# Delta in four operations, Q blocks from spread columns, 64-column scores and a new order of the first group in an attention backward kernel

## The chip, the cores and the metric

The kernel runs on one core of a Trainium2 chip. The metric is the device time of one execution in microseconds. The engines are PE (matrix multiplications, with weight loads listed apart as PEld), VectorE (DVE in the profile), ScalarE (ACT), GpSimd (POOL, which here issues the stores) and SyncE (SP, which issues the loads). Each engine works through its own instructions in order and waits on semaphores for the others.

## The reference

Two weights sets, A (attention over a cache) and B (an MLP), are each applied twice to the same small state x of shape 2 x 1 x 1024, and all gradients are returned:

```python
def _A_ref(x, k_cache, v_cache, wq, wo):        # Hq = 32, Hkv = 4, Sk = 16384, Dh = 128
    q = (x @ wq).reshape(B, Sq, Hq, Dh) ...
    scores = jnp.einsum("bhqd,bhkd->bhqk", q, k) * (Dh ** -0.5)
    p = _softmax(scores, axis=-1)
    o = jnp.einsum("bhqk,bhkd->bhqd", p, v)
    return (...o...) @ wo
...
    x = x + _A_ref(_layernorm(x), A_k_cache, A_v_cache, A_wq, A_wo)
    x = x + _B_ref(_layernorm(x), B_w1, B_b1, B_w2, B_b2)
    x = x + _A_ref(_layernorm(x), A_k_cache, A_v_cache, A_wq, A_wo)
    x = x + _B_ref(_layernorm(x), B_w1, B_b1, B_w2, B_b2)
    return x
...
_out, _vjp = jax.vjp(_f, A_x, A_k_cache, A_v_cache, A_wq, A_wo, B_w1, B_b1, B_w2, B_b2)
_grads = _vjp(grad_out)
```

For each of the 8 pairs of batch and KV head (a group, g) there are 8 query rows. The backward pass of attention needs, per layer, dO of the group, delta = the sum over the head of dO x O, ds = p x (V dO - delta), dq from ds and K, and the gradients dV = p dO and dK = ds q. dV and dK of the two layers are added and written once. The key and value caches and their gradients are 32 MB each.

## The kernel before

The kernel goes forward through both layers, then backward through layer 1 (`attn_bwd`, 500 to 662 us), and then through the MLP and attention of layer 0. The last part, from 731 us on, does layer 0's scores and dq and, for both layers together, dV and dK. It is the part that most of the change touches.

**Tiles.** A group has 16384 keys, cut into 4 chunks of 1 MB for K and 4 for V; a chunk is [128 partitions, 32 keys t, 128]. Chunk i of the last part is `chunks[i] = (group, c)`; `order` gives the groups, and the first one, `order[0]`, is group 7, whose K and V chunks were kept in SBUF (`held_tiles`, V already transposed). `e_all` holds the exponentials of both layers.

**Scores** (L1271). For 8 keys t, a transposed tile of V is the weight and the 16 columns of dO (two layers x 8 rows, `cols["V"]`) are streamed; the result goes to 16 places of a PSUM bank `dp` that lie 32 apart. A chunk has 32 such matmuls.

**ds** (`ds0`, L1276). One matmul of 512 columns with the weight `hot3` adds -delta to all of `dp`: `dlr` holds -delta as bf16 parts in three partitions, and `hot3` has ones in these three. VectorE then multiplies by `e_all` into `dX`.

**delta** (L859 to L882). VectorE multiplies dO by O, a matmul with ones sums over the partitions and gives the sum to every partition, and eight VectorE operations split it in three bf16 parts and put part i in partition i.

**Q blocks** (`make_qm`, L1211). For dV and dK, a weight block is a transposed piece of `e_all` or `dX`, and the streamed side is Qm, [128, 2 x 128], in which the 16 columns of dO or q are spread so that row 32r + 2k + t has column k in half t. PE transposes the 16 columns, VectorE copies them to `r16sb`, two matmuls with the constant `sel` spread them, and a copy brings them to SBUF. **`kv_pair`** (L1231) then makes half a chunk of dV or dK: 8 matmuls into four banks (`mx`), four copies out (`evac_cast`), and after the second half a store.

**dq** (`dq_quad`, L1297): 8 matmuls, four at a time in different columns of the array, with ds as weight and K streamed, into an accumulator. `evac` and `reduce` close a group.

**Banks and copies.** PSUM has two banks for transposes (`tp`), four for `mx`, one `sm` and one accumulator. `pick()` (L148) gives each copy out of PSUM to ScalarE or VectorE, by a planner's running charge of both; `charge` books other work.

**Order.** The program order of each engine is written by hand. After dO of layer 0 (`do_scaled`, L843; its products are ready at 731.5 us) the first group runs as a straight list (L1355 to L1388), then a loop over m (L1396) takes two slots of 8 keys x 128 per turn: transposes of V, scores two slots behind, `kv_pair`s for dK and dV, `make_blks`, a scheduled dq, and units of weight gradients (`step_fill`). Before, the list read: scores 1, delta's matmul, kv pair V 0, scores 2, delta, kv pair, scores 0, ds 1, scores 3, kv pair V 1, ds 0 and 2, dq of chunk 0, kv pair, ds 3, zeroing of two transpose banks (`fixed_tp`), K's Q block, dq of chunks 1 to 3. Loads wait in `pump` for tiles that are read or stored (`by_read`, `by_store`).

The w1 pass of layer 0 (`w_pass`, L1030) has a `mid` call that stands in PE's and VectorE's queues at its fifth chunk, at about 698 us.

Of the kernel before, what the change touches and what calls it, by code (L numbers as in the profile page):

```python
# [13 lines left out]
ALU = mybir.AluOpType  # L14
# [9 lines left out]
def kernel(  # L24
# [96 lines left out]
    sel = const.tile([16, 2, 4, 16, 2], BF16, name="sel")  # L121
    V.memset(sel[:], 0.0)
    for t in range(2):
        for r in range(4):
            V.tensor_copy(out=sel[:, t, r, :, t], in_=ident[0:16, 0:16])

# [5 lines left out]
    V.tensor_reduce(out=m3[:], in_=identf[:, 0:3], axis=AX.X, op=ALU.add)  # L132
# [701 lines left out]
    def attn_out_bwd(l, gT):  # L834
        V.tensor_copy(out=gA_all[:, :, lsl(l)], in_=gT[:])
        _, dops = w_pass(A_wo, HD, D, "do_ps", gT_bf=gA_all[:, :, lsl(l)])
        doT_bf = saved[f"a{l}"]["doT_bf"] = vec.tile([128, G, 8], BF16, name=f"doT_bf{l}")
        dof = do_scaled(l, dops)
        do_store(l, dof[:], doT_bf[:])
        delta(l, delta_mm(l, dof))  # L840
        return doT_bf

    def do_scaled(l, dops, ahead=None, half=lambda b, dof: None):  # L843
        sv = saved[f"a{l}"]
        dof = wrk.tile([128, G, 8], F32, name="dof")
        for b in (1, 0):
            V.tensor_tensor(out=dof[:, b * HKV:(b + 1) * HKV, :].rearrange("p k r -> p (k r)"), in0=dops[:, :, b],
                            in1=sv["rbc"][:, b * HKV:(b + 1) * HKV, :].rearrange("p k r -> p (k r)"), op=ALU.mult)
            if ahead is not None:
                r_ = sv["rbc"][:, b * HKV:(b + 1) * HKV, :].rearrange("p k r -> p (k r)")  # L850
                V.tensor_tensor(out=dof[:, b * HKV:(b + 1) * HKV, :].rearrange("p k r -> p (k r)")[:, 4:FJ:5],
                                in0=ahead.dp[:, :, b], in1=r_[:, 4:FJ:5], op=ALU.mult)
            half(b, dof)
        return dof
# [4 lines left out]
    def delta_mm(l, dof, bank=None):  # L859
        sv = saved[f"a{l}"]  # L860
        prod = wrk.tile([128, G, 8], F32, name="dprod")
        V.tensor_tensor(out=prod[:], in0=dof[:], in1=sv["oT"][:], op=ALU.mult)
        bank = pm_([128, 512], F32, "dl_ps") if bank is None else bank
        PE.matmul(bank[:, 0:G * 8], lhsT=onesf[:], rhs=prod[:].rearrange("p g r -> p (g r)"), start=True, stop=True)
        return bank

    def delta(l, bank):
        dlp = bank[:, 0:G * 8]
        rest_ = wrk.tile([128, G * 8], F32, name="dl_rest")
        V.tensor_scalar(out=rest_[:], in0=dlp, scalar1=-1.0, scalar2=None, op0=ALU.mult)  # L870
        part = wrk.tile([128, G * 8], BF16, name="dl_part")
        dst = dlr[:, :, l, :].rearrange("p g r -> p g r")
        as_g = lambda ap: ap.rearrange("p (g r) -> p g r", r=8)
        for i in range(3):
            V.tensor_copy(out=part[:], in_=rest_[:])
            if i == 0:
                V.tensor_scalar(out=dst, in0=as_g(part[:]), scalar1=identf[:, 0:1], scalar2=None, op0=ALU.mult)
            else:
                V.scalar_tensor_tensor(out=dst, in0=as_g(part[:]), scalar=identf[:, i:i + 1], in1=dst, op0=ALU.mult,
                                       op1=ALU.add)  # L880
            if i < 2:
                V.tensor_tensor(out=rest_[:], in0=rest_[:], in1=part[:], op=ALU.subtract)  # L882
# [138 lines left out]
    for w in "VK":  # L1021
        cols[w] = vec.tile([128, G, 2, 8], BF16, name="cols" + w)
        for k in range(2):
            if w + str(k) != "V0":
                V.tensor_copy(out=cols[w][:, :, k, :], in_=saved["a%d" % k]["qT_bf" if w == "K" else "doT_bf"][:])
    dq0 = vec.tile([128, G, 8], F32, name="dqT0")
# [5 lines left out]
                                  make_blks(0, None), make_blks(1, None)))  # L1032
# [176 lines left out]
    qms = {}  # L1209

    def make_qm(w, g):  # L1211

        rps = mtp()
        PE.transpose(rps[0:16, 0, :], cols[w][:, g].rearrange("p l r -> p (l r)"), ident[:])
        r16 = small.tile([16, 128], BF16, name="r16sb")
        V.tensor_copy(out=r16[:], in_=rps[0:16, 0, :])

        def second():
            Qm = wrk2.tile([128, 2, 128], BF16, name="Qm" + w)
            qps = mx()  # L1220
            for t in range(2):
                PE.matmul(qps[:, t * 128:(t + 1) * 128], lhsT=sel[:, t].rearrange("p r k t -> p (r k t)"), rhs=r16[:],
                          start=True, stop=True)
            evac_cast(Qm[:].rearrange("p a b -> p (a b)"), qps[:, 0:256], 256)
            qms[w, g] = Qm

        return second
# [43 lines left out]
    def scores(i, b, kT, dp):  # L1271
        do01 = cols["V"][:, chunks[i][0]].rearrange("p l r -> p (l r)")
        for j in range(8):
            PE.matmul(dp[:, :, b * 8 + j], lhsT=kT[:, j, :], rhs=do01, start=(b + j == 0), stop=False)
# [77 lines left out]
    def sm_dp():  # L1352
        return pm_([128, 16, TC], F32, "dp")[:]

    dof = do_scaled(0, pairs(dops, HQ), wob,  # L1355
                    lambda b, dof: do_store(0, dof[:, b * HKV:(b + 1) * HKV], cols["V"][:, b * HKV:(b + 1) * HKV, 0, :]))
    qv = make_qm("V", order[0])
    odp = {1: kept_scores(1, sm_dp())}
    dl_bank = pt([128, 512], F32, "dl")
    delta_mm(0, dof, dl_bank)  # L1360
    qv()
    kv_pair("V", 0, 0)
    odp[2] = kept_scores(2, tp_dp())
    delta(0, dl_bank)
    charge("D", 2.0)
    kv_pair("V", 0, 1)
    odp[0] = kept_scores(0, tp_dp())
    ds0(1, odp[1])
    odp[3] = kept_scores(3, sm_dp())
    kv_pair("V", 1, 0)  # L1370
    for c in (0, 2):
        ds0(c, odp[c])
    for q in range(2):
        dq_quad(0, q)
    kv_pair("V", 1, 1)
    ds0(3, odp[3])
    TP.extend(fixed_tp(i) for i in range(2))
    banks["tp"] = lambda: nxt("tp", TP)
    qk = make_qm("K", order[0])
    for c in (1, 2):  # L1380
        for q in range(2):
            dq_quad(c, q)
    qk()
    for q in range(2):
        dq_quad(3, q)
# [10 lines left out]
    while 2 * m < NS + 12 or late or fill or late_pe or m <= max(v_at) + 2:  # L1396
# [6 lines left out]
        for k in range(2):  # L1403
            s = 2 * m + k
            if s < NS:
                i, b = NCH + s // NB, s % NB
                cv = get("V", *chunks[i])[:].rearrange("p (t d) -> p t d", d=128)
                kT = ktp.tile([128, 8, 128], BF16, name="kT", tag="kT")
                tp = mtp()
                for j in range(8):  # L1410
                    PE.transpose(tp[:, j, :], cv[:, b * 8 + j, :], ident[:])  # L1411
                evac_bf16(kT[:].rearrange("p a b -> p (a b)"), tp[:].rearrange("p a b -> p (a b)"), 1024)
                kTs[s] = kT
                if b == NB - 1:
                    done("V", *chunks[i])
            if 0 <= s - 2 < NS:
                score0(s - 2)
# [46 lines left out]
```

## Time and profile before

| | |
|---|---|
| median of 9 runs | 1151.3 us (1146.68 to 1153.17) |
| the profiled execution | 1151.3 us |
| its span | 1149.5 us |
| mean granted TensorE clock | 0.834 |
| busy: PE, VectorE, ScalarE, GpSimd | 83%, 55%, 49%, 6% of the span |
| moved | 449.30 MB, mean 391 GB/s |

The page is of one execution. Busy shares are over the whole span. "PEclk" is the clock that TensorE was granted, 1.00 being full speed. The DMA share is the mean busy share of the core's 16 DMA engines. In a list of instructions in order of time, the first number is the start in us from the span's start, the second the duration, then engine, line, operation, output and inputs, shapes and count; a bracket gives the idle time before the instruction on its engine and what ended it. The end of a matmul is modelled, so a PE that is shown busy is not always one at its peak.

### The profile page before, as it was taken

Reading aid. Unit: us, or ns where it says so; the run is one execution under the profiler, and the core shown is the slowest. Engines: PE = TensorE matmul, PEld = TensorE weight load, DVE = VectorE, ACT = ScalarE, POOL = GpSimd, SP = SyncE. Lnnn points to the kernel's source line nnn. Section 1 sums busy time; section 2 is a strip of 40 time slices with the busy share of each in tenths; the row PEclk is TensorE's granted clock in tenths of the full one; section 3 lists DMA queues with packets and bytes.
Section 4 is the critical chain, followed back from the end, with each engine's and each line's share of the span. In section 5 each row is a group of like instructions: output and inputs, shape, how many; then the busy total and the mean of one; then the engine's idle time right before and its main releaser. Section 6 shows DMA issues by size and latency. Waiting matters only on the chain. (4 is left out here: it accounts for less than half of the span.)

```text
span 1149.5 us, 39958 instructions
## 1 busy us (share of the span) xinstructions
PE 953.5 (83%) x17581; PEld 727.6 (63%) x17581; DVE 632.1 (55%) x1335; ACT 567.2 (49%) x1417; POOL 63.9 (6%) x113
## 2 busy tenths in 40 slices
PE   4988886488879976899987799788898999998885
PEld 3867774487767755887775688665555555555552
DVE  1535441133535423454845365668777877787684
ACT  0544351022535420344454455657677867786673
POOL 0000000000000000000000000001111112111111
PEclk9979785597989876899998799888758867797695
DMA  8999999998999989999899899877999999999996
GB/s 371 424 424 424 424 424 412 409 361 363 424 424 424 423 328 423 405 355 411 345 420 421 324 370 351 323 291 291 397 402 408 422 422 420 424 422 420 423 423 260
DMA packets 89130, 449.30 MB, mean 391 GB/s; under 512 B 7026, under 2 KB 7026, under 8 KB 49788
## 3 DMA queue, kind: packets, MB, share of 16 engines
q1 hardware_dynamic: 72204, 348.17, 74.9%
q0 software_dynamic: 16752, 98.59, 20.7%
q8 instruction: 137, 2.24, 0.7%
q14 instruction: 37, 0.30, 0.1%
HBM read 348.14 MB, written 98.58 MB: 389 GB/s over the span
## 5 line engine op out<-in xcount | busy, mean ns | idle before, releaser
L158 ACT COPY kT<-tp 128x512 int32<-128x512 int32 x209 | 122.7, 588 | 257.5 <-PE tp L424 248.7
L161 DVE COPY kT<-tp 128x1024 bf16<-128x1024 bf16 x159 | 108.6, 690 | 109.6 <-PE tp L424 96.4
L424 PE MATMUL tp<-ident,kv_K 128*128 128x128 bf16 x1728 | 142.8, 231 | 4.0 <-DMA kv_K<-in_A_k_cache_dram 3.8
L424 PEld LDWEIGHTS <-kv_K 128*128 128x128 bf16 x1728 | 108.4, 103 | 4.7 <-DMA kv_K<-in_A_k_cache_dram 4.5
L169 DVE CAST big<-xm 128x512 bf16<-128x512 f32 x142 | 92.4, 685 | 29.9 <-PE xm L1242 12.9
L166 ACT CAST big<-xm 128x512 bf16<-128x512 f32 x155 | 84.6, 592 | 26.5 <-PE xm L1144 15.6
L577 PEld LDWEIGHTS <-kT 128*128 128x128 bf16 x2048 | 76.3, 98 | 28.1 <-issue 21.7
L577 PE MATMUL sc<-qT_bf,kT 128*128 128x8 bf16 x2048 | 91.8, 171 | 0.7 <-issue 0.7
L424 PE MATMUL tp<-ident,kv_V 128*128 128x128 bf16 x864 | 69.7, 226 | 13.6 <-DMA kv_V<-in_A_v_cache_dram 11.6
L274 PE MATMUL wtp<-ident,wt 128*128 128x128 bf16 x928 | 75.3, 228 | 3.9 <-issue 2.4
L541 ACT ACTIVATE e_all<-sc,negm 128x64 bf16<-128x64 f32 x256 | 77.1, 345 | 1.3 <-DVE negm L536 1.2
L310 PEld LDWEIGHTS <-wt 128*128 128x128 bf16 x1696 | 48.9, 103 | 43.8 <-issue 15.1
L169 DVE CAST keepK<-xm 128x512 bf16<-128x512 f32 x95 | 61.6, 684 | 15.5 <-PE xm L1242 9.8
L456 PE MATMUL acc_all<-kv_V,e_all 128*16 128x256 bf16 x864 | 46.3, 294 | 25.6 <-DMA kv_V<-in_A_v_cache_dram 13.1
L161 DVE COPY wT<-wtp 128x1024 bf16<-128x1024 bf16 (+1 forms) x64 | 40.5, 637 | 47.3 <-PE wtp L274 44.2
L158 ACT COPY wT<-wtp 128x512 int32<-128x512 int32 (+1 forms) x60 | 34.5, 575 | 63.4 <-PE wtp L274 48.3
L166 ACT CAST keepK<-xm 128x512 bf16<-128x512 f32 x102 | 54.8, 592 | 22.2 <-PE xm L1242 21.5
L424 PEld LDWEIGHTS <-kv_V 128*128 128x128 bf16 x864 | 54.8, 101 | 15.4 <-DMA kv_V<-in_A_v_cache_dram 12.3
L166 ACT CAST keepV<-xm 128x512 bf16<-128x512 f32 (+1 forms) x98 | 53.0, 592 | 21.9 <-PE xm L1242 18.7
L274 PEld LDWEIGHTS <-wt 128*128 128x128 bf16 x928 | 57.8, 102 | 4.7 <-issue 3.4
L541 ACT ACTIVATION_READ_ACCUMULATOR e_all<-sc,negm 128x1 f32 x256 | 60.2, 235 | 0.0
L169 DVE CAST keepV<-xm 128x512 bf16<-128x512 f32 (+1 forms) x74 | 47.9, 684 | 16.6 <-PE xm L1242 12.6
(352 smaller groups left out, 1777.8 us busy)
## 6 DMA issues: line engine op xcount, KB each, us to landing
kv_K<-in_A_k_cache_dram SPq DMA_DIRECT2D x81, 1024.0 KB, 12.2
kv_V<-in_A_v_cache_dram SPq DMA_DIRECT2D x81, 1024.0 KB, 12.2
out_dram<-big POOLq DMA_DIRECT2D x36, 1024.0 KB, 16.7
wt<-in_A_wo_dram SPq DMA_DIRECT2D x32, 1024.0 KB, 10.8
wt<-in_B_w_dram SPq DMA_DIRECT2D x32, 896.0 KB, 14.0
out_dram<-keepK POOLq DMA_DIRECT2D x22, 1024.0 KB, 16.8
out_dram<-keepV POOLq DMA_DIRECT2D x18, 1024.0 KB, 15.9
wt<-in_A_wq_dram SPq DMA_DIRECT2D x16, 1024.0 KB, 8.7
```

The costliest lines, as they stand in the source:

```text
L158: S.copy(out=dst.bitcast(I32), in_=src.bitcast(I32))
L161: V.tensor_copy(out=dst, in_=src)
L166: S.copy(out=dst, in_=src)
L169: V.tensor_copy(out=dst, in_=src)
L274: PE.transpose(tp[:, o, :], wv[:, j, (o0 + o) * 128:(o0 + o + 1) * 128], ident[:])
L310: PE.matmul(fps[:, jo, :].rearrange("p (a b) -> p a b", b=2), lhsT=wv[:, j, jo * 128:(jo + 1) * 128], rhs=xT_bf[:, j0 + j, :].unsqueeze(1) ...
L424: PE.transpose(tp[:, j, :], cv[:, b * 8 + j, :], ident[:])
L456: PE.matmul(self.acc[cg:cg + 16, :], lhsT=coef(u), rhs=self.cv[:, t:t + 2, :].rearrange("p t d -> p (t d)"), start=False, stop=True, tile_ ...
L541: S.activation(out=e_all[:, g, f * half:(f + 1) * half, l, h, :], in_=sc[g][f][:, h, :].rearrange("p (a b) -> p a b", b=2), func=ACT.Exp, ...
L577: PE.matmul(sc[g][f][:, :, t % TH], lhsT=kT[:, j, :], rhs=q_bf[:, g, :], start=True, stop=True)
```

## The change

Delta is split by four VectorE operations in place of eight: every partition gets the first part, partitions 64 to 127 are overwritten with the second, and 96 to 127 with the third; `hot3` has its ones in partitions 0, 64 and 96. For layer 0 it is done in two halves of the groups, the second half first.

A Q block is made from the columns spread by VectorE into a zeroed tile `spr` (two copies), used as the weight of two matmuls with the identity. The transpose, `r16sb` and `sel` are gone. K's block of the first group, and what is known of V's, are made inside the w1 pass (`q_parts`).

Scores stream 64 columns: a tile `wide_do` has the 16 columns of dO at every seventh place with zeros around them, and each matmul of key t writes a run of four keys, of which it adds zero to three. Two such tiles alternate by group; a copy per group fills one.

The first group's list is reordered: the dq of a chunk follows its ds, between the kv pairs, and the other half of delta is made near the end.

```diff
-    V.tensor_reduce(out=m3[:], in_=identf[:, 0:3], axis=AX.X, op=ALU.add)
+    V.tensor_reduce(out=m3[:], in_=identf[:, 64:128:32], axis=AX.X, op=ALU.add)
+    V.tensor_tensor(out=m3[:], in0=m3[:], in1=identf[:, 0:1], op=ALU.add)
...
-    def delta(l, bank):
-        dlp = bank[:, 0:G * 8]
-        rest_ = wrk.tile([128, G * 8], F32, name="dl_rest")
...
-        for i in range(3):
-            V.tensor_copy(out=part[:], in_=rest_[:])
...
+    def delta(l, bank, gs=slice(0, G)):
+
+        dlp = bank[:, 8 * gs.start:8 * gs.stop].rearrange("p (g r) -> p g r", r=8)
+        rest_ = wrk.tile([128, G, 8], F32, name="dl_rest")[:, gs]
+        dst = dlr[:, gs, l, :]
+        V.tensor_scalar(out=dst, in0=dlp, scalar1=-1.0, scalar2=None, op0=ALU.mult)
+        V.scalar_tensor_tensor(out=rest_, in0=dlp, scalar=-1.0, in1=dst, op0=ALU.mult, op1=ALU.subtract)
+        V.tensor_copy(out=dst[64:128], in_=rest_[64:128])
+        V.tensor_tensor(out=dst[96:128], in0=rest_[96:128], in1=dst[96:128], op=ALU.subtract)
...
+    for w in "VK":
+        spr[w] = wrk.tile([128, 258], BF16, name="spr" + w)
+        nc.gpsimd.memset(spr[w][:], 0.0)
+
+    def q_spread(w, gcols, k0, n):
+        diag = spr[w][:].rearrange("p (t x) -> p t x", x=129)[:, :, 0:128].rearrange(
+            "p t (r k z) -> p t r k z", r=4, k=16)[:, :, :, k0:k0 + n, 0]
+        for t in range(2):
+            V.tensor_copy(out=diag[:, t], in_=gcols.unsqueeze(1).to_broadcast([128, 4, n]))
+
+    def q_make(w, g, bank):
+        Qm = wrk2.tile([128, 2, 128], BF16, name="Qm" + w)
+        for t in range(2):
+            PE.matmul(bank[:, t * 128:(t + 1) * 128], lhsT=spr[w][:, t * 128:(t + 1) * 128], rhs=ident[:],
+                      start=True, stop=True)
+        evac_cast(Qm[:].rearrange("p a b -> p (a b)"), bank[:, 0:256], 256)
+        qms[w, g] = Qm
+
+    def q_parts():
+        q_spread("K", cols["K"][:, g0_].rearrange("p l r -> p (l r)"), 0, 16)
+        q_make("K", g0_, px([128, 512], F32, "qk0"))
+        q_spread("V", cols["V"][:, g0_, 1, :], 8, 8)
+        V.tensor_copy(out=wide_do[g0_][:, 8:16, 3], in_=cols["V"][:, g0_, 1, :])
+
+    do_tiles = [vec.tile([128, 16, 7], BF16, name="wdo%d" % i) for i in range(2)]
+    for t in do_tiles:
+        nc.gpsimd.memset(t[:], 0.0)
...
-                                  make_blks(0, None), make_blks(1, None)))
+                                  make_blks(0, None), make_blks(1, None), q_parts()))
...
     def make_qm(w, g):
...
+        q_spread(w, cols[w][:, g].rearrange("p l r -> p (l r)"), 0, 16)
+        return lambda: q_make(w, g, mx())
...
     def scores(i, b, kT, dp):
-        do01 = cols["V"][:, chunks[i][0]].rearrange("p l r -> p (l r)")
+        wd = wide_do[chunks[i][0]]
         for j in range(8):
-            PE.matmul(dp[:, :, b * 8 + j], lhsT=kT[:, j, :], rhs=do01, start=(b + j == 0), stop=False)
+            t, x = b * 8 + j // 4 * 4, 3 - j % 4
+            PE.matmul(dp[:, :, t:t + 4], lhsT=kT[:, j, :], rhs=wd[:, :, x:x + 4], start=(b + j == 0), stop=False)
...
+    do_scaled(0, pairs(dops, HQ), dof, wob, (1,))
+    dl_bank = delta_mm(0, dof, pt([128, 512], F32, "dl"), halves[1])
+    q_spread("V", dof[:, g0_], 0, 8)
+    q_make("V", g0_, mx())
+    V.tensor_copy(out=wide_do[g0_][:, 0:8, 3], in_=dof[:, g0_])
     odp = {1: kept_scores(1, sm_dp())}
...
+    do_scaled(0, pairs(dops, HQ), dof, wob, (0,))
+    delta(0, dl_bank, halves[1])
+    charge("D", 1.0)
     kv_pair("V", 0, 0)
+    odp[0] = kept_scores(0, tp_dp())
+    for c in (1, 0):
+        ds0(c, odp[c])
+    kv_pair("V", 0, 1)
     odp[2] = kept_scores(2, tp_dp())
...
+    for q in range(4):
+        dq_quad(1 - q // 2, q % 2)
     odp[3] = kept_scores(3, sm_dp())
+    for c in (2, 3):
+        ds0(c, odp[c])
     kv_pair("V", 1, 0)
...
+    for q in range(4):
+        dq_quad(2 + q // 2, q % 2)
+    dl_bank = delta_mm(0, dof, pt([128, 512], F32, "dl"), halves[0])
     kv_pair("V", 1, 1)
+    do_store(0, dof[:], cols["V"][:, :, 0, :])
+    delta(0, dl_bank, halves[0])
     TP.extend(fixed_tp(i) for i in range(2))
...
+                if b == 0 and chunks[i][1] == 0:
+                    wg = chunks[i][0]
+                    V.tensor_copy(out=wide_do[wg][:, :, 3], in_=cols["V"][:, wg].rearrange("p l r -> p (l r)"))
```

## The prediction, made before the result was known

> **What bounds the kernel now.** The profiled execution has a span of 1149.5 us and took 1151.3 us with what lies around it (1.8 us). That is the median of the nine runs too, so the sum below needs no scaling. I read the page's slices first, then the stretches where the DMA engines are not full, then the instructions in order of time there, then the chain that ended last.
>
> The page's slices show the DMA at 8 or 9 tenths nearly everywhere and its rate at its lowest (291 GB/s) around 780 us. Cut into 4 us stretches (columns: busy us of PE, weight loads, VectorE, ScalarE and GpSimd with counts; granted clock; DMA share; GB/s):
>
> ```profile
> core 0: us, PE busy (x) PEld busy (x) DVE busy (x) ACT busy (x) POOL busy (x), PEclk, DMA share, GB/s
> 732.00:736.00 4.00, 3.12 (x79) 2.43 (x80) 2.17 (x9) 1.45 (x3) 0.00 (x0) 1.00 1.01 424
> 736.00:740.00 4.00, 2.58 (x62) 1.76 (x62) 2.47 (x10) 2.05 (x4) 0.58 (x1) 0.53 0.26 109
> 740.00:744.00 4.00, 2.90 (x43) 0.98 (x40) 2.48 (x4) 1.07 (x2) 0.00 (x0) 0.50 0.64 246
> 744.00:748.00 4.00, 1.92 (x30) 1.09 (x30) 0.91 (x2) 3.06 (x6) 0.54 (x1) 0.50 0.69 252
> 748.00:752.00 4.00, 4.00 (x58) 2.82 (x48) 0.42 (x1) 0.83 (x2) 0.00 (x0) 0.50 0.63 264
> ...
> 760.00:764.00 4.00, 3.27 (x55) 1.99 (x47) 3.54 (x7) 3.11 (x7) 0.16 (x1) 1.00 0.11 43
> ...
> 784.00:788.00 4.00, 3.87 (x44) 2.36 (x44) 3.26 (x6) 2.91 (x6) 0.53 (x1) 0.57 0.32 137
> ...
> 792.00:796.00 4.00, 3.78 (x47) 2.04 (x45) 3.19 (x6) 3.06 (x7) 1.25 (x3) 0.79 1.00 412
> ```
>
> Up to 736 and from 792 to about 1124 the DMA share is 1. In between, (1 - share) x 4 us over all stretches sums to 19.6 us of missing transfer time. No engine waits for a transfer there: prefetched tiles lie ready, and stores and loads wait for engines to fill and free tiles. So between 731 and 792 us the engines set the pace, after 792 the transfers do. The chain that ended last crosses the later part on DMA (27, 30 and 22 us pieces up to 1081), then on engines. A microsecond saved before 792 lets every later transfer start earlier and should reach the end.
>
> The first group's work, 731.57 to the loop's first transposes at 750.42, in order of time:
>
> ```profile
> 731.57 0.19 DVE L847 TENSOR_TENSOR dof<-wob_b,rbc 128x32 f32<-128x32 f32 x1 [1.44 <-PE wob_b L385]
> ...
> 738.03 0.58 PE L1278 MATMUL dp<-dlr,hot 128*128 128x512 bf16 x1 [0.60 <-DVE dlr L879]
> 739.40 1.02 PE L1274 MATMUL dp<-colsV,keepV 128*128 128x16 bf16 x32 [0.78 <-DVE keepV L1282]
> ...
> 743.04 1.03 PE L456 MATMUL acc_all<-keepK,keepV 128*16 128x256 bf16 x16 [1.10 <-DVE keepV L1282]
> ...
> 747.24 0.27 PE L1214 MATMUL tpm<-ident,colsK 128*16 128x128 bf16 x1 [2.08 <-ACT tpm L1339]
> ...
> 750.42 1.89 PE L1411 MATMUL tpm<-ident,keepxV 128*128 128x128 bf16 x16
> ```
>
> PE stands still for delta, for the first ds, for a ds again and for a transpose bank (the brackets), and from 736.3 to 753.3 runs at half clock: a quad (8 matmuls of 256 columns, L456) comes every 0.5 us here, against 0.22 us at full clock at 770 (0.40 with 0.18 of drain).
>
> **The clock.** In the trace it changes in steps of 3.41 us. I added the streamed columns of each step, each weighted by the share of the array it uses (a 16-column weight counts 1/8). In 19 of 20 steps the next clock is full if the sum was above about 2,600 and half if below. The step from 732.9 had 1,967, the three after it 1,239 to 2,023. A 64-column score raises the sum: a group of 32 counts 2,048 instead of 512.
>
> **Part by part.**
>
> Layer 1's delta (501 us): eight dependent VectorE operations at L870 to L882 take 500.34 to 502.44; four of 0.2 us take 0.9. The next kT copy starts 1.2 us earlier, for which PE waits:
>
> ```profile
> 503.43 0.36 PE L676 MATMUL dp<-doT_bf,kT 128*128 128x8 bf16 x8 [1.12 <-DVE kT L161]
> ```
>
> DMA share there is 0.79, so it counts: **-1.1** (0 if the PE-bound stretch at 550-560 or the DMA after it takes it back; -1.2 at most).
>
> Constants at the start: 8 copies and a memset (2.42 to 3.32 us) go, one 0.17 us addition comes. DMA is full from 4 us on: 0 (uncovered: -0.7).
>
> q_parts inside the w1 pass (at 700 us): two spreads for K, two matmuls, one copy of 256 columns, two spreads and a small copy for V. On PE's queue the two matmuls wait for the spreads, which stand on VectorE behind the blkv copy that ends 700.80: 700.80 + 2 x 0.2 = 701.2, where PE would have gone on at 700.43, so 0.8 plus 2 x 0.057. Behind them are the pass's transposes, and PE is 7.93 of 8 us busy in 704-712. **+0.9** (0.1 if later slack absorbs it, 1.8 if the VectorE's extra 1 us delays a wT copy as well). The four memsets on GpSimd stand ahead of one store; that queue had been waiting for 264 us. SP's queue is not touched here.
>
> The first group, from 731.57, at rows of full clock:
> - two dof operations and the half product (pitch 0.21 each): PE at 732.23. Delta's product (0.44, half as wide) and two Q matmuls: 732.7. The 0.37 us Q copy ends 733.3 beside the scores. The transpose, r16sb and the wait of 0.46 are gone.
> - scores of chunk 1: 32 x 30 ns = 0.96 (the row of 16 columns, 732.38 to 733.34): 733.7; kv pair 0.2, scores of chunk 0 0.96: 734.9. Delta's four operations end at 733.7, so the 0.60 wait is gone. Two ds matmuls 0.43; their VectorE products (0.69 each) end 736.0 and 736.6.
> - the second kv pair waits until ScalarE has emptied three banks (734.1 + 3 x 0.55): 735.8; scores of chunk 2: 737.0; four quads x 0.22: 737.9; scores of chunk 3: 738.9; two ds: 739.3; kv pair: 739.5.
> - the last quads wait for the ds products (740.0, 740.7): 741.1. Then comes a wait the change adds: the other half's delta matmul waits on PE for a VectorE copy and the product (741.5); behind it stand the last kv pair and the loop. 0.44 more: 742.0; kv pair 742.2; two ScalarE copies to 743.45, the zeroing of a transpose bank 0.57: the loop starts at 744.1.
> Against 750.42: **-6.3**. The steps from 732.9 on then count over 5,000, so the clock should hold. At half clock the two later score groups cost 0.7 more each, the eight quads 0.28 each (half of it under the waits for ds), kv pairs and ds 0.5 in all: 3.0 less gain, -3.3. That is the small end; -7.0 the large (the last two waits overlap).
>
> Here one rule weighs against the change. The trace gives 26 to 30 ns per 16-column score at either clock (0.21 us per 8 at half clock). It has no 64-column matmul: nearest are 32 columns, 30 ns, and 128 columns, 57 ns full and 101 half. The Trainium skill, "TensorE: Matmul & The Clock Gate", section "Back-to-back issue gap", has a floor of about 25 ns up to 64 columns at full clock, but N / 1.2 GHz at half. So 64 columns would be free warm (29 ns) and double cold: 53 ns. The row's proportion (101 / 2 = 50) says the same. Taking the 16-column row everywhere, the loop's scores cost nothing; by the rule each slot of 8 costs +0.2 us cold, +0.02 warm. I use the rule.
>
> The loop's first iteration ran at half clock, with two transpose groups of 0.8 us: at full clock **-1.2** (0 to -1.7). Second iteration at 754.88 before, about 747.4 after.
>
> Loop to 792: one change of group there. VectorE gets two more spreads and one copy (+0.6), loses the wait of PE for a transpose bank and r16sb (0.8 at 772.5): +0.4 with the delay of the copies behind. Scores, warm: 14 slots x 0.02 = +0.3. SP's loads wait for the stores of V1 and V2, which come 1 and 3 us earlier. Together **+0.7** (-0.5 to +1.5).
>
> Tail from 1081 (engines): two score groups at half clock +0.4, one group change -0.1: **+0.3** (0 to +1).
>
> Sum: -1.1 + 0.9 - 6.3 - 1.2 + 0.7 + 0.3 = **-6.7**: 1151.3 - 6.7 = **1144.6 us**.
>
> **Rivals.** About 0.2% (2.3 us) is what can be told from no change.
> - Slower: cold scores make PE the bound where the DMA is it now. From 800 to 1100 the clock is half in about 48% of the time, and some 100 slots pass: 100 x 0.48 x 0.21 = +10 us on PE, whose idle time there is 30 us (the busy column against the stretches). For it: PE is at 91%. Against: the scores add some 410 to a step's sum, which lifts steps that stood at 2,200 over 2,600; and PE's time has room. It decides if less than a third of the idle time can be used. 1144.6 + 10 = 1154.6 (1152 to 1157): 0.20.
> - The clock falls anyway in the first group: -3.3 and no -1.2: 1148.8 (1147 to 1150): 0.12.
> - Given back: the loop to 792 is paced by tiles coming free, and the missing DMA time only moves. For it the 0.11 at 760-764; against it, engines there wait for each other and not for DMA. Only layer 1 and w1 stay: 1151.1 (1149 to 1153): 0.12.
> - More: fewer half-clock steps also at 784 and 794, where PE is 3.8 of 4 us busy: -3 more: 1141.6 (1140 to 1142.5): 0.08.
> - The sum as worked out: 1144.6 (1142.5 to 1147): 0.48.
>
> Faster: 0.48 + 0.08 + 0.07 of the second = 0.63. Within: 0.05 + 0.11 + 0.01 = 0.17. Slower: 0.20. The range 1141.5 to 1153 leaves out half of "more" and three quarters of "slower", 0.19; the likeliest case alone has 1142.5 to 1147.
>
> **What would show it.** Right: first loop transposes about 12.5 us after the first dof product (18.85 before), granted clock 1.00 in that stretch, the missing DMA time down from 19.6 to some 13 us, share 1 from about 785 on; the wait of 1.12 at L676 gone; PE held under 1 us by the Q matmuls in the w1 pass. Wrong: PE near 4.0 of 4 us with a DMA share under 0.95 after 800, a score group of 8 at over 0.4 us there, or the loop starting early and the share still under 1 until 792.

## The result and the profile after

The changed kernel takes 1156.8 us (median of 16 runs, 1152.0 to 1160.9) against 1151.0 us for the kernel before (53 runs): ratio 1.0044 with a 95% interval of [1.0033, 1.0055]. (Ratios are worked out from the single runs, with their intervals, and differ a little from the quotient of the medians.) It is slower by 5 to 6 us, where 1144.6 was forecast. Its profiled execution has a span of 1155.8 us and a mean granted clock of 0.840, against 1149.5 and 0.834.

The first group, as the trace of the changed kernel has it in order of time (start, duration, engine, line, operation, shapes, and in brackets what the engine waited for):

```profile
743.98 0.19 DVE L844 TENSOR_TENSOR dof<-wob_b,rbc 128x32 f32<-128x32 f32 x1 [1.12 <-PE wob_b L380]
...
745.07 1.21 PE L1275 MATMUL dp<-wdo,keepV 128*128 128x64 bf16 x32
...
749.73 1.05 PE L451 MATMUL acc_all<-keepK,keepV 128*16 128x256 bf16 x32
...
754.38 0.38 PE L855 MATMUL dl<-dprod,onesf 128*128 128x32 f32 x2 [0.17 <-DVE dprod L853]
...
756.73 0.61 PE L1412 MATMUL tpm<-ident,keepxV 128*128 128x128 bf16 x8 [1.65 <-ACT tpm L1340]
```

From the first dof product to the loop's first transposes it is now 756.73 - 743.98 = 12.75 us (12.5 forecast, 18.85 before). Four quads (L451, 32 matmuls) take 1.05 us, which is full clock. From the first dof product to the end it is 1155.8 - 743.98 = 411.8 us, where it was 1149.5 - 731.57 = 417.9. So the part behind the first dof product gained 6.1 us, nearly what the forecast has for it (-6.3 - 1.2 + 0.7 + 0.3 = -6.5).

The loss lies ahead of it, nearly all in code that was not changed: the first dof product comes at 743.98 and not at 731.57, 12.4 us late. Of these, 11.7 us are there at layer 1's first dof product already (510.89 and not 499.17). The page's rate of the DMA engines in 40 slices shows where; first the kernel before, then the changed one:

```profile
GB/s 371 424 424 424 424 424 412 409 361 363 424 424 424 423 328 423 405 355 411 345 420 421 324 370 351 323 291 291 397 402 408 422 422 420 424 422 420 423 423 260
```

```profile
GB/s 369 417 418 418 419 418 398 397 357 341 418 418 417 418 324 386 397 371 394 372 415 409 361 347 345 332 311 306 401 417 423 420 417 420 410 422 419 424 423 255
```

In the forward part, whose slices held 424 GB/s, they hold 418 now. The stretches of that part (busy us of PE, weight loads, VectorE, ScalarE, GpSimd with counts; clock; DMA share; GB/s) say what kind of loss it is; the kernel before, then the changed one:

```profile
20.00:60.00 40.00, 32.83 (x726) 30.15 (x726) 17.02 (x35) 15.55 (x51) 0.00 (x0) 1.00 1.01 424
320.00:360.00 40.00, 34.42 (x689) 28.00 (x686) 18.39 (x42) 18.31 (x80) 0.00 (x0) 0.91 1.01 424
```

```profile
20.00:60.00 40.00, 31.82 (x705) 29.05 (x706) 15.99 (x33) 15.20 (x50) 0.00 (x0) 0.98 1.01 418
320.00:360.00 40.00, 34.13 (x683) 27.63 (x679) 19.17 (x42) 17.79 (x83) 0.00 (x0) 0.91 1.01 418
```

The share is 1.01 in both, so no engine holds the transfers up: the same transfers take longer. In the trace, the 8 KB load packets between 60 and 150 us took 309 ns before (tenth, fiftieth and ninetieth percentile all 309, mean 310.4) and take 311, 312 and 319 ns now (mean 315.4). The 2 KB load packets between 150 and 240 us took 84.4 ns on average and take 88.4. So a packet costs some 4 to 5 ns more whatever its size, and the rate falls most where packets are small (412 and 409 GB/s to 398 and 397 in the seventh and eighth slice). Up to layer 1's first dof product the same 202.3 MB keep the 16 engines busy for 492.9 us before and 502.8 us now (the durations of all packets, divided by 16). These 9.9 us are most of the 11.7; executions of the same code scatter there by some microseconds.

What did the diff do to loads that it does not touch? It drops the constant `sel` (512 bytes per partition) and adds two `wdo` tiles (2 x 224 bytes). The large tiles behind them move down by 64 bytes. In the compiled programs the tiles that the loads fill begin at byte 58880 of a partition before (230 x 256) and at 58816 after, 192 past a multiple of 256.

### The profile page after: what moved, and what is told of

Read it like the earlier page. It is cut to its first block, busy times and chain, and to the rows that moved or that the text cites. A ratio compares the mean times of both kernels' runs of the same rounds, so it can differ in the third digit from the quotient of the medians.

```text
span 1155.8 us, 39972 instructions
## 1 busy us (share of the span) xinstructions
PE 957.8 (83%) x17567; PEld 741.6 (64%) x17567; DVE 633.3 (55%) x1347; ACT 566.7 (49%) x1418; POOL 64.7 (6%) x117
## 5 line engine op out<-in xcount | busy, mean ns | idle before, releaser
L419 PE MATMUL tp<-ident,kv_K 128*128 128x128 bf16 x1728 | 146.5, 235 | 5.4 <-DMA kv_K<-in_A_k_cache_dram 4.9
L419 PEld LDWEIGHTS <-kv_K 128*128 128x128 bf16 x1728 | 111.0, 105 | 6.4 <-DMA kv_K<-in_A_k_cache_dram 5.6
L164 DVE CAST big<-xm 128x512 bf16<-128x512 f32 x135 | 87.9, 685 | 27.3 <-PE xm L1160 12.6
L161 ACT CAST big<-xm 128x512 bf16<-128x512 f32 x162 | 88.4, 593 | 26.3 <-PE xm L1160 15.2
L305 PEld LDWEIGHTS <-wt 128*128 128x128 bf16 x1696 | 48.9, 103 | 44.3 <-issue 15.6
L164 DVE CAST keepK<-xm 128x512 bf16<-128x512 f32 x91 | 59.0, 685 | 22.4 <-PE xm L1242 17.5
L451 PE MATMUL acc_all<-kv_V,e_all 128*16 128x256 bf16 x864 | 47.5, 301 | 28.3 <-DMA kv_V<-in_A_v_cache_dram 15.5
L161 ACT CAST keepV<-xm 128x512 bf16<-128x512 f32 (+1 forms) x93 | 50.3, 594 | 18.8 <-PE xm L1242 15.7
L164 DVE CAST keepV<-xm 128x512 bf16<-128x512 f32 (+1 forms) x80 | 52.3, 685 | 12.3 <-PE xm L1242 9.2
## 6 DMA issues: line engine op xcount, KB each, us to landing
kv_K<-in_A_k_cache_dram SPq DMA_DIRECT2D x81, 1024.0 KB, 12.4
```

Source lines behind the costliest of these rows:

```text
L161: S.copy(out=dst, in_=src)
L164: V.tensor_copy(out=dst, in_=src)
L305: PE.matmul(fps[:, jo, :].rearrange("p (a b) -> p a b", b=2), lhsT=wv[:, j, jo * 128:(jo + 1) * 128], rhs=xT_bf[:, j0 + j, :].unsqueeze(1) ...
L451: PE.matmul(self.acc[cg:cg + 16, :], lhsT=coef(u), rhs=self.cv[:, t:t + 2, :].rearrange("p t d -> p (t d)"), start=False, stop=True, tile_ ...
```

## The experiments

Theory A: the slower loads come from where their tiles begin, and with the 64 bytes back the kernel takes what was forecast. Rival B: they come from the change itself (its zeroed tiles, its order, the chip). A second question came up on the way: which part of the change gives the 6 us.

**64 bytes back.** An unused constant after `zero1`, in the changed kernel:

```diff
+    pad0 = const.tile([128, 16], F32, name="pad0")
+    V.memset(pad0[:, 0:1], 0.0)
```

> The changed kernel with one unused tile of 64 bytes per partition ahead of all large tiles, so that the tiles that loads fill start at multiples of 512 bytes again, as in the kernel before (58880); in the changed kernel they start at 58816, 64 bytes lower. Theory A (addresses: the 12 us by which the trace after is late at the start of layer 0's first group come from load packets that take longer at the shifted addresses): 8 KB packets are back at 309 ns, the forward part moves 424 GB/s, first dof product at about 731 us, and the time is 1151 - 6 = 1145 us, ratio 0.995 to before. Theory B (the code of the change itself slows it, through the w1 pass or the 64-column scores on PE): the pad changes nothing, 1156 to 1157 us. Theory C (the profiled execution after was only slower by chance in its first part): 1150 to 1157 with a forward part anywhere between.

1144.9 us, ratio 0.9943 [0.9921, 0.9966] to the kernel before. The page's rate:

```profile
GB/s 371 424 424 425 425 424 412 409 373 357 423 425 419 424 308 420 400 365 407 370 423 418 351 375 356 317 332 313 390 421 423 418 421 422 423 422 420 423 423 248
```

424 is back, and the 8 KB packets take 310.4 ns. A holds.

**The kernel before, moved.** The same two lines in the kernel before, with 448 bytes (192 past 256, as in the changed kernel) and with 256:

> The kernel before with one unused tile of 448 bytes per partition, so that its load tiles start at 448 past a multiple of 512, as in the changed kernel. Nothing else is changed. Theory A: 12 us slower than before in the first 731 us and some more behind, 1161 to 1163 us, ratio 1.010. Theories B and C: 1151, ratio 1.000.

> The kernel before with one unused tile of 256 bytes per partition: load tiles start at 256 past a multiple of 512. Theory A with a grid of 256 bytes (the Trainium skill, DMA: Bandwidth & Descriptors, How a descriptor splits into AXI transactions: a descriptor that does not start on a 256-byte boundary is read from the boundary below, one more transaction): no change, 1151. Theory A with a grid of 512 bytes: 1157 to 1163. Theory B: 1151, so this run tells only what the grid is, given the second run.

448 bytes: 1163.1 us, ratio 1.0099 [1.0078, 1.0120]. 256 bytes: 1150.7 us, 0.9997 [0.9985, 1.0010]. The first one's rate:

```profile
GB/s 370 418 418 418 420 418 398 396 361 345 417 420 414 418 308 417 389 358 403 376 413 410 346 361 364 311 303 277 369 413 420 414 417 420 418 421 419 423 423 272
```

So the place alone costs 1.0% in a kernel in which nothing else is changed, and B is out as a cause of this loss.

**Which tiles.** The changed kernel with 64 bytes ahead of the constants' users and 448 more behind the pool of kT, the blocks, dX and Qm, so that only `e_all`, the load tiles and the kept tiles (which loads fill and stores read) begin at multiples of 256:

```diff
+    pad0 = const.tile([128, 16], F32, name="pad0")
...
+    pad1 = ktp.tile([128, 112], F32, name="pad1", tag="pad1", bufs=1)
```

> The changed kernel with 64 unused bytes ahead of the large tiles and 448 behind the load and kept tiles: only the exponentials and the tiles that transfers fill or empty are back on multiples of 512; the transposed tiles kT, the blocks, dX and Q blocks stay at 448 past one, as in the changed kernel. Theory A (transfers): 1145 us, as the run with 64 bytes alone. Rival A2 (the addresses matter to the engines' reads and copies of kT and the blocks, not to the transfers): 1155 to 1157.

1146.0 us, ratio 0.9953 [0.9937, 0.9970], 8 KB packets 310.5 ns: where kT, the blocks, dX and Qm begin doesn't matter. `e_all`, which only engines touch, was not separated from the load tiles, but what got longer is the load packets themselves.

**How far off.** The kernel before with 64 and with 128 bytes:

> The kernel before with 64 unused bytes: load tiles start 64 past a multiple of 256. 192 past it cost +12.8 us. Rule of the Trainium skill (DMA: Bandwidth & Descriptors, How a descriptor splits into AXI transactions): bytes below the start down to the boundary are moved too, (8192 + 64) / 8192 = 0.8% more beats against 2.3% at 192: a third of the cost, about +4, 1154 to 1155 us. Rival (one more transaction per packet, whatever its size): the same cost as at 192, 1162 to 1164 us. A third: only 448, that is 64 below a multiple of 512, is bad: 1151.

> The kernel before with 128 unused bytes: load tiles start 128 past a multiple of 256. By the beats of that rule two thirds of the cost at 192: +8.5, about 1159 us. By one more transaction per packet: 1162 to 1164. By a grid of 128 bytes: 1150 to 1151.

1162.9 us (1.0108 [1.0087, 1.0129]) and 1162.8 us (1.0098 [1.0074, 1.0122]); 8 KB packets 315.2 and 314.6 ns (315.2 with 448 bytes, 192 past 256). 64, 128 and 192 bytes cost the same. The Trainium skill, "DMA: Bandwidth & Descriptors", section "How a descriptor splits into AXI transactions", says that a descriptor is cut at multiples of 256 bytes, and that one that starts between them also pays for the bytes below its start. It words this for bytes that are fetched; here it is the side that is written. The grid of 256 agrees with the runs. That the price would grow with those bytes doesn't: as an estimate from that page it would be 0.8, 1.6 and 2.3% of an 8 KB packet (2, 4 and 6 more beats of 32 bytes to 256); measured are 1.5, 1.4 and 1.6%. For 2 KB packets the same estimate is 3.1, 6.2 and 9.4%; measured are 88.0, 88.3 and 88.4 ns against 84.4, that is 4.3, 4.6 and 4.7%. A fixed price of some 4 to 5 ns per packet, whatever the distance and the size, fits both. That it is one more piece per packet is a guess; no run here shows the pieces.

**The 64 columns.** The 64 bytes back, and scores that stream 16 columns again:

```diff
-            t, x = b * 8 + j // 4 * 4, 3 - j % 4
-            PE.matmul(dp[:, :, t:t + 4], lhsT=kT[:, j, :], rhs=wd[:, :, x:x + 4], start=(b + j == 0), stop=False)
+            PE.matmul(dp[:, :, b * 8 + j], lhsT=kT[:, j, :], rhs=wd[:, :, 3], start=(b + j == 0), stop=False)
```

> The changed kernel with the 64 unused bytes (load tiles on multiples of 512) and the scores streaming 16 columns again, in the same order of the list: each matmul writes one key's 16 places, the weight is the same. Theory K (the 64 columns hold the clock and that is worth time): the clock falls to half inside the first group, the loop starts 1 to 3 us later than with 64 columns (12.9 us after the first dof product) and the time is 1147 to 1149. Theory L (64 columns only cost PE time in half-clock stretches; the gain is all from the order): 1144 or less, first group 12.5 to 12.9 us.

1143.6 us, ratio 0.9939 [0.9920, 0.9958]: with the new order, the 64 columns are worth nothing that can be measured.

**Delta alone.** The kernel before with the four-operation delta, in one piece:

> The kernel before with only delta's new split (four operations, all groups at once, ones of hot3 in partitions 0, 64, 96); load tiles stay on multiples of 512. Step of the prediction: -1.1 at 501 us and up to -0.6 for the wait at 738: 1149 to 1150 us, the wait of 1.12 us at the first scores after 503 us gone. Rival: what is won at 501 is given back before 660, 1150 to 1151.

1155.1 us, ratio 1.0037 [1.0021, 1.0052]: slower, which no theory had. Its first dof product comes at 730.2, but from there to the end it takes 423.1 us instead of 417.9. Two more runs take this apart, with four copies of delta's result onto itself, which bring back about its old length (layer 0's delta ends 6.2 us after the first dof product, 6.4 before, 5.5 with delta alone), in both layers (shown) and in layer 0 alone:

```diff
+        for _ in range(4):
+            V.tensor_copy(out=dst, in_=dst)
```

> The kernel before with the delta of four operations, and behind it four copies of its result onto itself, in both layers, so that delta takes about as long as the eight operations did. The four operations alone gave 1155.1 us, 0.37% slower than before. If the shorter delta, by starting the last part 1.4 us earlier, brings a worse order of loads, stores and clock there: 1151 us, as before. If the form of the split does it (the parts in other partitions, or the small tiles that moved by 128 bytes): 1155 us again.

> As the kernel before with the four-operation delta, with the four idle copies in layer 0 alone: only layer 1's delta is shorter. If the start of the last part, 1.1 us earlier, is what costs: 1155 us. If it is the shorter delta within the first group, where the scores and ds then follow otherwise: 1150 us, the saving of layer 1 and nothing else.

1150.0 us (0.9991 [0.9979, 1.0004]) and 1150.3 us (0.9998 [0.9985, 1.0011]). So layer 1's shorter delta neither gains nor costs anything that can be told, and it is layer 0's that costs, by its timing and not by its form: 0.7 us earlier in the first group, 4 to 5 us later at the end. Late stretches of the kernel with delta alone, then of the one with copies in layer 0:

```profile
1075.00:1080.00 5.00, 4.76 (x49) 2.42 (x48) 3.30 (x6) 3.23 (x6) 1.83 (x3) 0.50 1.01 426
1085.00:1090.00 5.00, 5.00 (x59) 3.40 (x57) 3.54 (x6) 2.75 (x6) 1.31 (x2) 0.50 1.01 425
1120.00:1125.00 5.00, 3.83 (x44) 1.64 (x41) 3.58 (x7) 3.22 (x6) 0.76 (x2) 0.50 0.59 249
```

```profile
1075.00:1080.00 5.00, 3.40 (x27) 1.55 (x20) 1.38 (x2) 1.76 (x3) 0.76 (x1) 0.54 1.02 429
1085.00:1090.00 5.00, 3.94 (x62) 3.01 (x63) 3.59 (x8) 3.09 (x6) 0.55 (x1) 0.90 1.01 421
1120.00:1125.00 5.00, 3.20 (x20) 2.06 (x20) 2.38 (x7) 2.08 (x5) 0.00 (x0) 0.50 0.93 393
```

With delta alone PE goes through 1065 to 1090 at half clock and 4.8 to 5.0 of 5 us busy, and by 1120 the share of the transfers is down to 0.59. In the other PE has idle time at 1075, a clock of 0.90 at 1085, and a share of 0.93 at 1120. That the slow stretch of PE is what costs the time is read from one trace of each and not tested; why an earlier delta leads to it stays open.

**The order of the first group.** The 64 bytes back and 16 columns, but the first group in the old order with delta in one piece; four-operation delta and new Q blocks stay. Then the opposite: the kernel before with the new order alone.

```diff
-    do_scaled(0, pairs(dops, HQ), dof, wob, (1,))
+    do_scaled(0, pairs(dops, HQ), dof, wob, (1, 0))
...
     kv_pair("V", 0, 0)
-    odp[0] = kept_scores(0, tp_dp())
-    for c in (1, 0):
-        ds0(c, odp[c])
+    odp[2] = kept_scores(2, tp_dp())
+    delta(0, dl_bank)
...
```

> The changed kernel with the 64 bytes restored and 16-column scores (1143.6 us), but the first group in the order of the kernel before, with delta in one piece; the four-operation delta and the new Q blocks stay. If the order is what gains: the loop starts some 16 us after the first dof product and not 12.9, 1147 to 1150 us. If delta and the Q blocks gain: 1144 us. Since the four-operation delta alone in the kernel before made it slower (1155.1), 1153 is possible as well: then the order only repairs what the shorter delta costs.

> The kernel before with the new order of the first group alone, dof and delta in halves; eight operations for delta, the old Q blocks and 16-column scores stay, and the load tiles are where they were. The prediction put most of its 6.3 us down to this order. If the order gains by itself: about 1147 us. If it gains nothing, as the run without it suggests (1143.3 against 1143.6 us with it): 1151 us.

Old order: 1143.3 us, ratio 0.9933 [0.9920, 0.9947], no worse than with the new order (0.9939). New order alone: 1150.5 us, 0.9995 [0.9978, 1.0013]. The order gains nothing that can be told, though the second interval leaves room for 2.5 us. Yet it does start the loop earlier. After the first dof product, the loop's transposes come at +15.6 us with the old order (745.30 - 729.71) and at +12.7 with the new one. What becomes of the 2.9 us is seen in the stretches, first new order (16 columns), then old order:

```profile
776.00:780.00 4.00, 2.81 (x51) 1.90 (x50) 3.19 (x6) 3.33 (x8) 0.00 (x0) 1.00 0.81 326
780.00:784.00 4.00, 3.90 (x39) 1.55 (x36) 3.75 (x7) 3.30 (x7) 0.53 (x1) 0.55 0.49 207
784.00:788.00 4.00, 4.00 (x58) 2.96 (x57) 2.75 (x5) 2.25 (x5) 0.53 (x1) 0.60 0.57 174
```

```profile
736.00:740.00 4.00, 2.94 (x43) 1.18 (x41) 1.80 (x3) 1.48 (x3) 0.58 (x1) 0.50 0.57 242
740.00:744.00 4.00, 3.17 (x49) 1.42 (x53) 2.17 (x5) 1.57 (x4) 0.00 (x0) 0.50 0.58 186
...
776.00:780.00 4.00, 3.34 (x51) 1.89 (x49) 3.54 (x7) 3.27 (x8) 0.53 (x1) 1.00 0.34 141
780.00:784.00 4.00, 3.93 (x67) 2.86 (x66) 4.00 (x8) 3.50 (x8) 0.53 (x1) 1.00 0.68 246
784.00:788.00 4.00, 3.72 (x62) 2.28 (x60) 3.58 (x7) 3.58 (x8) 1.06 (x2) 1.00 0.89 246
```

The old order has the half clock in the first group, and then full clock from 748 on. The new order is at full clock there (728 to 744) and has the lower clock in the loop, around 750 and at 780 to 788. The missing DMA time from 728 to 800 is 12.4 us with the old order and 13.4 with the new: it moved. Whether a half clock is what holds that time at all is asked below.

**The Q blocks alone, and 64 columns with the old order.** The run with the old order, with the eight-operation delta besides; and with the 64-column scores besides.

> The changed kernel with the 64 bytes restored, of which only the new Q blocks are left: delta in eight operations and in one piece, 16-column scores, the first group in the order of before. The run with delta in four operations besides gave 1143.3 us. If the Q blocks are the gain, because no transposing is left in the first group and at a change of group: 1144 us (delta's own 1 to 2 us, which the kernel before could not use, lost again). If the gain needs both: 1148 to 1151 us.

> The changed kernel with the 64 bytes restored and the first group in the order of before; 64-column scores, four-operation delta and new Q blocks stay. With 16 columns this order gave 1143.3 us. If 64 columns hold the clock where the old order let it fall to half (732 to 745 us at 0.50): 1141 us. If their price on PE shows in the loop: 1145 to 1148 us. If neither: 1143 us.

Q blocks alone: 1146.6 us, ratio 0.9958 [0.9940, 0.9975], against 0.9933 with the shorter delta; the intervals overlap, so delta's share beside the Q blocks stays small and unsure. 64 columns with the old order: 1142.8 us, 0.9930 [0.9908, 0.9952], the same time as with 16. The clock, however, is not the same. These are its stretches, to be held beside those of the old order above:

```profile
736.00:740.00 4.00, 3.22 (x76) 2.42 (x75) 3.40 (x8) 2.62 (x5) 0.50 (x1) 1.00 0.67 277
740.00:744.00 4.00, 2.47 (x58) 1.54 (x57) 2.41 (x4) 1.07 (x2) 0.08 (x1) 1.00 0.63 266
...
776.00:780.00 4.00, 2.87 (x51) 1.94 (x48) 3.19 (x6) 3.33 (x8) 0.00 (x0) 1.00 0.71 293
780.00:784.00 4.00, 3.49 (x54) 1.92 (x51) 3.87 (x8) 3.38 (x7) 0.53 (x1) 1.00 0.59 248
784.00:788.00 4.00, 3.72 (x53) 2.02 (x49) 4.00 (x7) 4.00 (x9) 0.96 (x2) 1.00 0.57 150
```

The granted clock is 1.00 in every stretch from 728 to 792, where with 16 columns it was 0.50 from 732 to 744; over six runs of each kernel the median of the mean clock is 0.855 against 0.838. The loop starts at +14.2 us and not at +15.6. Yet the missing DMA time is 11.6 us against 12.4, and the time is the same. So a full clock can be had in this whole part, and the transfers are hardly less late for it: the half clock is not what holds most of the missing time there.

**Fewer waits.** The 16-column kernel with three waits moved: the spreads of `q_parts` to the front of the `mid` call, the other half of delta between the first scores, one transpose bank zeroed early.

```diff
+    delta_mm(0, dof, dl_bank, halves[0])
     odp[0] = kept_scores(0, tp_dp())
+    delta(0, dl_bank, halves[0])
...
     odp[2] = kept_scores(2, tp_dp())
+    TP.append(fixed_tp(0))
```

> The changed kernel with the 64 bytes restored and 16-column scores (1143.6 us), and three waits moved: K's and V's spreads stand ahead of the work that kept PE waiting 0.77 us in the w1 pass; the other half of delta is made between the first scores instead of at the end; the first transpose bank is zeroed early, so that the loop's first transposes don't wait 1.64 us for it. If what is saved before 792 us reaches the end, as the prediction has it: 0.8 + 1.6 + 0.4 less, 1140.8 us. If tiles coming free hold the transfers in this part, the missing DMA time only moves: 1143.6 us, the same.

1144.8 us, ratio 0.9951 [0.9935, 0.9968]: nothing more. The loop starts at +12.0 and the missing DMA time to 800 us is 10.6, with about 1 more behind it; it doesn't come through to the time.

The traces in one table, worked out from their rows (us; "missing" is the sum of (1 - DMA share) x 4 us over 728 to 800):

| kernel | first dof product | loop's first transposes, after it | missing | first dof product to end | median |
|---|---|---|---|---|---|
| before | 731.6 | 18.9 | 19.6 | 417.9 | 1151.0 |
| before + 256 bytes | 731.8 | 18.9 | 18.0 | 418.5 | 1150.7 |
| before + 448 bytes | 740.8 | 18.9 | 18.4 | 419.1 | 1163.1 |
| delta alone | 730.2 | 18.5 | 17.8 | 423.1 | 1155.1 |
| new order alone | 732.9 | 15.2 | 18.3 | 415.8 | 1150.5 |
| Q blocks alone, aligned | 734.0 | 15.8 | 14.0 | 412.8 | 1146.6 |
| Q blocks and delta, aligned | 729.7 | 15.6 | 12.4 | 410.9 | 1143.3 |
| the same and new order | 732.2 | 12.7 | 13.4 | 411.7 | 1143.6 |
| the changed kernel, aligned | 729.9 | 12.9 | 12.0 | 411.5 | 1144.9 |
| Q blocks and delta and 64 columns, aligned | 732.9 | 14.2 | 11.6 | 410.2 | 1142.8 |
| the changed kernel | 744.0 | 12.8 | 15.4 | 411.8 | 1156.8 |

"Aligned" means load tiles at multiples of 256. For the two moved kernels the window of "missing" starts too early, since their first group begins 9 to 12 us later; in the same place relative to the first dof product the changed kernel has 13.7. The aligned kernels' first dof product scatters by 4 us between executions (729.7 to 734.0) in nearly the same code, so one trace tells nothing of 2 us there. The last column but one is steadier: four traces of the kernel before or near it (with 256 bytes, and with the old length of delta) lie within 417.9 and 418.6. By this measure the new order alone has 2.1 us less behind the first dof product, which its median doesn't show.

## Why the prediction was wrong

**The step that failed: what was left out.** The sum starts from 1151.3 and takes all code ahead of layer 1's delta as unchanged. The change's part on the constants was costed at 0 by its instructions (8 copies and a memset less, under transfers that are full from 4 us on); that a constant of 512 bytes goes, and that this moves every load tile, was never asked. It is 11 to 13 us by the padded kernels before (1.0%), some 4 to 5 ns on every load packet, against a forecast gain of 6.7. None of the rivals had it: the slower one rested on cold 64-column scores, and the runs with and without the 64 columns are equal.

**The sum of the changed part, -6.7, was right as a sum.** With the 64 bytes back the kernel takes 1144.9 us, where 1144.6 was forecast, and missing DMA time is 12.0 us where 13 was. That the total fits so well is luck in part, because its terms are another matter:

- First group, -6.3: the loop starts 12.75 us after the first dof product, 12.5 forecast. But the rule behind it, that a microsecond saved before 792 reaches the end, holds for half of it. The 3 us that the Q blocks save there come through, with some 2 more in the loop (418 to 412.8 us, one trace of each). The 2.9 us of the new order don't, as far as can be told. The prediction's "given back" rival was right for this part, and it wasn't split by parts of the change.
- The Q blocks' weight was hidden in one line of that term ("the transpose, r16sb and the wait of 0.46 are gone"). With the old ones the kernel before waits 2.08 us for a zeroed bank to transpose K's columns; with the new ones the quads go on. What they save later in the loop wasn't separated further.
- Layer 1's delta, -1.1: the wait of 1.12 at its first scores is gone, as forecast; the line has no bracket any more in the changed kernel:

```profile
513.21 0.36 PE L671 MATMUL dp<-doT_bf,kT 128*128 128x8 bf16 x8
```

  The time isn't there: with layer 1's delta alone shortened the ratio is 0.9998 [0.9985, 1.0011], which leaves at most 1.7 us. Where it went is not shown: from layer 1's first dof product to layer 0's the aligned traces with the long delta take 228.4 to 232.4 us, those with the short one 228.5 to 231.0, and one microsecond can't be told in that scatter.
- q_parts, +0.9: the wait is 0.77 us, 0.8 forecast:

```profile
712.62 0.33 PE L1026 MATMUL qk<-ident,sprK 128*128 128x128 bf16 x2 [0.77 <-DVE sprK L1021]
```

  The run that takes it away (with two other waits) is no faster.
- First iteration at full clock, -1.2: not so in the changed kernel, which has the half clock again in the loop's first iteration (with the old order the clock is full there, and the time is no better):

```profile
752.00:756.00 4.00, 2.68 (x52) 1.24 (x51) 2.76 (x6) 2.45 (x5) 0.00 (x0) 1.00 0.56 223
756.00:760.00 4.00, 2.94 (x28) 2.66 (x27) 2.17 (x8) 2.56 (x6) 0.54 (x1) 0.74 0.87 307
760.00:764.00 4.00, 4.00 (x58) 3.45 (x57) 0.86 (x2) 0.67 (x2) 0.00 (x0) 0.50 0.61 233
```

- 64 columns: the price at full clock was small, as forecast (32 scores in 1.21 us against 1.03 with 16 columns, some 6 ns more for each), and at half clock from one score to the next it is 53 ns (median of 294 in the aligned kernel), as the prediction has it. The clock behaves as forecast too. The prediction's sum of columns, added up anew over the whole trace of the kernel before (a matmul that lies in two steps is shared between them), is on the side of 2,600 that goes with the next clock in 313 of 328 steps. With the old order and 16 columns the first group's steps count 1,649 to 2,362 and run at half clock; with 64 columns they count 3,072 to 4,433 and run at full clock. With the new order the clock there is 1.00 with 16 columns already. What fails is that a clock held up is worth time: with the old order, where the 64 columns do hold it up, the time is the same.
- Slower by a PE at half clock: not by 64 columns. Something like it may stand behind the kernel with delta alone, where PE at half clock from 1065 to 1090 goes with 4 to 5 us lost; that this is the cause was not tested.

## What to carry to other kernels

A diff that adds or drops a tile can move all tiles behind it: where loads alone set the pace, look at where their tiles begin in memory before and after, and pad to a multiple of 256 bytes. If code that was not changed gets slower at the same DMA share, look at the duration of single packets. And time saved on a path that engines and transfers share in turns must be traced to the end for each part of a change by itself; here the new order gave nothing that can be told, and what was a single line of the sum (the Q blocks) gave most.

## What the runs showed of the hardware that was not expected

- A load into SBUF that starts 64, 128 or 192 bytes past a multiple of 256 costs the same in each case: 418 GB/s instead of 424, and 1.0% of this kernel. 256 bytes further costs nothing. The price is per packet and not per byte: 4 to 5 ns on 310 for 8 KB, 4 ns on 84 for 2 KB.
- The price falls ahead of the last part, where mostly loads fill the engines: there it is 8 to 12 us (first dof product at 739.4 to 743.5 in the moved kernels before, 731.6 to 731.8 in the others). In the last part, where loads and stores share them, 418.2 to 419.2 us against 417.9 to 418.6: at most 1.3. The 8 KB load packets have the same median and ninetieth percentile there, 309 ns between 900 and 1000 us, with and without the shift, although the tiles are no better placed; why is not shown.
- A low clock can move instead of going away: with the new order the half-clock stretch left the first group and came back in the loop, around 750 and 780 us. And a clock that is full throughout need not save time: with 64 columns and the old order it was 1.00 from 728 to 792 us, at the same 1143 us.
- An earlier start of a part can make it longer: four fewer operations in layer 0's delta cost 0.37% in one arrangement, and in another (with the new Q blocks) cost nothing.
